# A gated linear attention and token/channel mixer kernel: some transposes moved from TensorE to transposing DMAs, with a new order of the program

## The chip, the cores and the metric

The kernel runs on one core of a Trainium2 chip. The metric is the device time of one execution in microseconds (us): lower is better, and the median of several executions is compared. A profile is one execution of the same program recorded by the hardware profiler.

The engines named below: TensorE (PE; its weight loads are listed as PEld) does matmuls and transposes, VectorE (DVE), ScalarE (ACT) and GpSimd (POOL) do elementwise work, SyncE (SP) issues DMAs. TensorE writes into eight PSUM banks only; VectorE and ScalarE take results out of them (an "eviction").

## What is computed

Four batches, 8 heads, 768 tokens, head size 48. First a recurrence with decay for each head, then an MLP mixer over tokens and over channels (d_tok 256, d_ch 1536, width 8 x 48 = 384):

```python
for t in range(S):
    state = alpha[:, :, t, :, None] * state + einsum('bhd,bhe->bhde', k[:, :, t], v[:, :, t])
    y[:, :, t] = einsum('bhd,bhde->bhe', q[:, :, t], state)
x = y.transpose(0, 2, 1, 3).reshape(B, S, H * D)
h = maximum(x.transpose(0, 2, 1) @ w_tok1, 0) @ w_tok2
u = x + h.transpose(0, 2, 1)
out = u + maximum(u @ w_ch1, 0) @ w_ch2
```

Inputs and output are float32; matmul operands in the kernel are bfloat16.

## The kernel before

The recurrence is done in chunks of 128 tokens, six to a batch, numbered 0 to 23 over the four batches (batch 2 has chunks 12 to 17). For a chunk done alone (`natural_chunk`; batch 0 and the first four chunks of batch 1 go in pairs, `paired_chunks`) the steps are:

- four loads on SP's queue: alpha, k, q, v of the chunk, 192 KB each (`natural_loads`, line 203);
- ScalarE: la = ln(alpha) (line 241); TensorE: cum, its running sum over the tokens, with four columns of totals (lines 345 and 348); ScalarE: ek = exp(-cum) and eq = exp(cum) (lines 254 and 256);
- POOL: the decayed keys pkk = k x ek and queries pkq = q x eq, and v cast to bfloat16 (lines 273 and 280);
- `s_transpose` (line 290): 16 TensorE transposes of 64x64 blocks (`row_tiles`, line 287) put pkk and pkq, transposed, into two PSUM banks, and two evictions (line 295) bring them to the tile tkq, [128, 2, 4, 128];
- gt: the products of keys and queries (line 362), masked on VectorE into gm (line 302); state (line 383) and its decay and sum (st, ss, lines 312 to 319); y = gm x v and the part from the state before (lines 395 and 331), evicted to x (line 326).

With a batch's six x tiles the mixer runs: tok1 (two groups of six matmuls, line 574) and relu to ht; tok2 (line 623) for each chunk, added to x on VectorE, which makes u (line 629). Then u is transposed in two halves of three chunks: 18 TensorE transposes a half (step `utp`, `row_tiles` again), and two evictions a half (line 641) into ut, [128, 3, 768]. (Batch 0 makes u's transpose directly by matmuls, `mixed`.) The channel mixer `channel` then does ch1 (24 groups of three matmuls that read ut, line 663; each evicted with relu to rt, lines 561 and 563) and ch2 (groups of four, line 687), adds u on VectorE (line 700) and stores 192 KB per chunk from SP's queue (line 703).

Every step is put into a list with `g.add` and is numbered by its place in it. The order in which the steps are issued is written out in the string `ORDER`: the step's number, after a point the PSUM banks that it uses, and a letter where the engine is chosen (A for ScalarE, D for VectorE, P for POOL). `f` and a digit is a filling matmul on zeros (line 762), which keeps TensorE busy where it would have nothing to do. A loop at the end emits the steps in this order; each engine runs its own in that order, and semaphores between the engines are added by the framework. All DMAs of the program take eight completion counters in turn, in the order of the string, so a DMA's issue also waits until the DMA eight places before it has landed. The costs given to `g.add` (such as `{"PE": 0.25}`) are a planner's and do nothing in the program.

So TensorE mixes the channel matmuls of one batch with the chunks of the next: while batch 2's chunks run, batch 1's ch1 and ch2 stand between their steps.

Of the kernel before, what the change touches and what calls it, by code (L numbers as in the profile page):

```python
# [16 lines left out]
N_BANKS = 8  # L17
FETCH, BLOCK, AHEAD, ARRIVES = 193, 256, 449, (4.5, 30.0, 3.0)

# [4 lines left out]
0 1 f0 2 f0 f0 f0 f0 f0 3 f0 f0 f0 f0 f0 4 28 f0 29 f0 f0 30.0 5 31.1 32 f2 f2 38 6 f2 35 f2 33 f2 f2 f2 39 f2 36 f2  # L24
40 f2 43.2 41 7 47.3 66 f4 34 f4 65 48 44 50A 49D f4 68.4 8 45A 67.5 46D 75 f6 51.67 69 77 54.10 76 53 f3 9 f3 70 f3
55 f3 72 f3 f3 f3 73 f3 f3 f3 78 f3 105 84.3 80.2 52 104 81 10 85 56 83A f7 106.7 42P 37A 86D 107.1 87A f4 11 82D
57.46 108 71 88.03 114 59 111 58.25 109 12 90 115 61 63 60A 116 f4 62 119.4 64A f3 89 91.32 14 f6 93 120 f6 f6 122A f6
112 f6 f6 121A f6 117 123.6 f5 92 79A 74P f5 16 124 f5 110 f5 125A 126D 94.50 18 96 113A 118P 127.24 97 130.13 20
95.76 129 13A 100 24 128 98 102 133.5 99A 101 142.4 131 166.2 135 15A 141.7 143 132 144 146 169.0 145 136 17A 134.13
259 103D 137 139 19P 147 138A 163.5 140D 148 f6 150 152 149 151 162A 172.6 178.1 161D 175.3 f4 f4 164 170 21A 22D 23P  # L30
167 260 165D 179 171A 176 168D 180A 173 177D 189.4 261 174A 181.7 190D 187.5 26A 27P 182D 191.0 262 188D 25A 197.2
192D 185.1 198D 153 217.3 186A 213.6 263 218D 221.4 264 214D 155 207.7 222D 265.5 208D 215.0 300 267 227.2 268 216D
270 266.1 228D 201.3 273 271 205.6 274 202D 203.4 206A 301 272 211.7 204A 275 193.5 154A 212D 195.0 302 194D 276 183.2
196D 209.1 184D 277 278.36 303 279 210A 269 223.4 156P 280D 281A 292.75 224A 157 282 283 294 225.0 284A 285D 199.2 304
296 219.1 159 305 200D 286.47 226A 297 289.36 220A 287 307.5 343 306.2 291 315 234.0 314 288 317 308 290 229.1 309 316
293.46 344 310 239.5 313 295A 158D 345 311 298 249.7 299A 346 312 160A 250 366 318 230 333.23 367 347 319.46 320 335
251 322A 368 321D 336 240 252A 369 235 339 348.2 340 253 231 349 354 350 236 232D 352 370 241 237D 233 351 323 353 324
242A 371.7 238 325D 326A 361.3 243 244.2 372 362 486 373 375 327.10 487 330.56 328 355.43 245 376 356A 488 331 357A
246 329 374 489 377 378.71 332 247A 358.45 254.3 379A 508 360 380A 359 255 490 381.02 334.67 248 382 337 364.5 383
338A 363 256 509 365A 510 341 384.1 257A 342D 491.4 497 385A 511 492 388.0 493 495 258 386.2 389D 512 496 531 532  # L40
504.6 513.5 387A 494 498.37 505 514 394.1 533 500A 499D 390.4 517 395 515 392.0 396.2 391 400.6 518 393 398.3 534
501.71 397 516 402.54 519 399 520.02 404A 554 403D 526.3 521A 401 412.5 522A 555 502 448.4 535 527 405.60 449A 556
523.27 503 528 536.3 407A 436.4 524 406A 557 506.1 537 525 428.0 538 438.2 577 540 507D 437A 529.6 413D 429A 444.7 578
439A 539 530D 542 446.3 558 445D 541 549.1 408.4 447A 550 410.5 409D 551 579 559.0 411A 442.2 561 440.6 580 443D 560
564 424.7 441A 454.3 600 425A 563 422.1 581 455D 420.4 601 423A 562 582.5 565 421A 543.02 602 584 566.67 544D 572.3
545A 416.1 567D 585 603 568A 573 434.4 587 583 430.0 435D 417A 720 546.62 574 431A 569.37 548 432.5 721 588 604 426.1
547 586 433A 450.4 722 571 427A 552.0 451A 570 605.2 723 553A 418.6 606 575.5 419D 607 452.7 609 576A 414.1 453A 461.4
742 610 415A 724 466.3 743 611 589.06 608 612.25 591A 590D 744 595.7 476.1 614D 613A 596 481.0 745 597 615.65 592.27
765 617 482 731 593 766 462 746 594 477 767 616 598.5 478 768 599A 618.2 479 456.7 788 619A 753 457 620.6 769 480
622.5 621A 789 458 623A 790 467 459 776 791 628.1 632.2 629 626.6 460 624.5 633 630.7 627 634.1 792 811 468 631 812  # L50
625 471.2 635 813 472 469 636.67 470 639.51 638A 637D 473 640D 799 641A 814 483 474 834 463 484 725.3 475 464 747.6
726 770.7 666.5 727 729 465 749 793.1 667D 678.2 748 485 771 728 648.0 730 679D 794 646.4 649D 795 664.3 815 751 835
647D 656.5 772 836 665D 816.6 752 657A 760.2 670.1 837 817 738.0 818 750 658.4 671D 774 838 732.73 739 659A 754.56
734D 839.1 773 733A 775 761 783.0 755A 684.4 756D 841 644.3 762 685D 840 668.7 645D 797 676.2 784 669A 682.5 677A 785
777.64 683A 757.13 778D 735.07 779A 796 662.2 798 759 652.5 737 663A 822 654.6 653A 736 820 800.43 655A 780.27 758
740.5 802A 819 806.0 781 843 686.6 741A 763.1 782 687A 829.3 842 688.2 764A 807 844 786.5 801D 689A 650.7 808 787D
803.61 651A 846.04 821 804 672.2 847A 805 674.5 848A 845 680.7 830 673A 849.60 675A 831 823.14 681A 851 809.3 824A
660.2 825D 810A 850 642.5 661A 710.7 643A 711 852.0 690.1 853A 700.4 826.36 691 828 705.2 827 706 707 832.5 708 701
833A 709 702 854.0 703 704 856.6 855A 692 857A 695.3 693 860.2 694 868.5 861 858.4 696 869 859 862.0 864.6 863 697 865
866.1 698 715.2 867 699 716 873.54 870.06 874A 875D 717 872D 882.3 871D 712 718 883A 719 884.1 713 904.4 885A 714  # L60
896.5 905A 914.6 897A 886.0 915A 902.2 887A 878.3 903A 916.7 879A 910.1 917A 912.4 911A 920.5 913A 890.6 921A 918.0
891A 880.2 919A 892.3 881A 898.7 893A 894.1 899A 876.4 895A 888.5 877A 944.6 889A 922.0 929.2 923A 900.3 908.7 901D
906.1 909A 930 907A 939.4 945 946 934.5 947 935 948 936 931 937 924.0 938 932 925 933 926 940 927 941 928 949.3 942
950 943 951 954.7 955 952 956 953 957 958
# [12 lines left out]
class Graph:  # L77
# [5 lines left out]
    def add(self, name, costs, emit, reads=(), writes=(), prio=0, dma=None, new=(), tail=0.0, rows=False, loose=False, n=0):  # L83
        self.ops.append(Op(costs, emit, new))
        return self.ops[-1]
# [6 lines left out]
def kernel(  # L92
# [96 lines left out]
    for t in la_t + pkq_t + pkk_t:  # L189
# [615 lines left out]
```

## Time and profile before

| | us |
|---|---|
| median of 3 runs (lowest, highest) | 174.58 (173.62, 174.63) |
| the profiled execution's own time | 174.98 |
| its span, first to last instruction | 173.2 |
| TensorE transposes of pkk, pkq and x in `row_tiles` (line 287), instructions | 112 + 112 + 108 |
| evictions of them: tkq on ScalarE / VectorE | 18 x 0.594 / 10 x 0.418 |
| evictions of them: ut on ScalarE / VectorE | 6 x 0.642 / 6 x 0.450 |
| POOL: pkk, pkq, each | 1.000, 1.029 |
| input load of a chunk, issue to landing, medians | 4.2 to 4.6 |

Lengths of matmuls in the group rows overlap (a 384-column matmul is listed with 326 ns, but the next starts 163 ns later); the pieces of the chain of work do not overlap, and prices of matmuls are best read there. In the slices, each digit is a tenth of the slice's 4.33 us. In the waits, the engine and line before the arrow waited for those behind it. "To landing" is from a DMA's issue to the arrival of its completion.

### The profile page before, as it was taken

The numbers are of one execution on the slowest core, as the hardware profiler recorded it, in microseconds if no ns is written. First come the engines' busy times: TensorE is split into PE (matmuls) and PEld (weight loads), VectorE is DVE, ScalarE is ACT, GpSimd is POOL, SyncE is SP. The second block draws the span as 40 slices with busy tenths as digits, with TensorE's granted clock in tenths as the row PEclk, the third lists the DMA queues.
The fourth block names the chain that finished last, engine by engine and source line by source line (L and its number), as shares of the span: only waits on it lengthen the run. The fifth ranks groups of instructions, "written<-read, shape, count | busy, mean of one in ns | idle before, by whom it ended". The sixth has DMA issues, their size and how long they took to land.

```text
span 173.2 us, 5139 instructions
## 1 busy us (share of the span) xinstructions
PE 166.3 (96%) x2095; PEld 106.1 (61%) x2095; DVE 98.8 (57%) x207; ACT 101.5 (59%) x213; POOL 70.7 (41%) x112
## 2 busy tenths in 40 slices
PE   7989799999999999899999999999999999999993
PEld 3667477555665666566566666666766666656662
DVE  3259786976843585697482718687972257101141
ACT  2577664757845767498896331688891212895000
POOL 7432511419494944928766111499950000000000
PEclk9999999999999999999999999999999999999999
DMA  5999999999999999989898999987000121200133
GB/s 139 261 262 265 251 338 406 285 262 315 244 312 169 204 250 186 237 159 200 162 193 141 206 165 218 229 228 132 0 4 0 45 95 45 91 4 0 44 119 109
DMA packets 86150, 30.20 MB, mean 174 GB/s; under 512 B 79600, under 2 KB 85104, under 8 KB 86128
## 3 DMA queue, kind: packets, MB, share of 16 engines
q1 hardware_dynamic: 86128, 29.89, 74.6%
q8 instruction: 16, 0.26, 0.7%
q14 instruction: 6, 0.05, 0.1%
HBM read 25.17 MB, written 4.72 MB: 172 GB/s over the span
## 4 chain that ended last, share of the span: by engine, by line
PE 69%; DMA 13%; issue 4%; SPq 4%; ACT 4%; POOL 3%; DVE 1%; ACTq 0%; POOLq 0%; DVEq 0%
PE bank L687 24%; PE bank L663 20%; DMA ina<-in_alpha_dram 9%; DMA rt_late<-in_moe_w_ch_dram 4%; SPq L203 4%; PE bank L762 3%; PE bank L287 2%; PE bank L623 2%; PE bank L574 2%; PE bank L362 2%; PE bank L493 2%; PE bank L331 1%; ACT la L241 1%; PE bank L395 1%; PE bank L554 1%
## 5 line engine op out<-in xcount | busy, mean ns | idle before, releaser
L663 PE MATMUL bank<-ut,wc 128*128 128x384 bf16 x288 | 51.8, 326 | 0.0
L663 PEld LDWEIGHTS <-wc 128*128 128x128 bf16 x288 | 26.4, 98 | 16.2 <-ACT wc L728 0.2
L273 POOL TENSOR_TENSOR pkk<-ink,ek 128x384 bf16<-128x384 f32 x24 | 23.9, 1000 | 15.6 <-ACT ek L254 13.2
L687 PE MATMUL bank<-wc,rt 128*128 128x384 bf16 x144 | 26.9, 326 | 0.2 <-ACT wc L734 0.2
L687 PE MATMUL bank<-wc,rt_late 128*128 128x384 bf16 (+2 forms) x156 | 25.2, 314 | 0.0
L561 ACT ACTIVATE rt_late<-bank 128x384 bf16<-128x384 f32 x40 | 19.2, 496 | 4.0 <-PE bank L663 4.0
L302 DVE TENSOR_TENSOR gm<-bank,u 128x512 bf16<-128x512 f32 x28 | 17.7, 682 | 5.8 <-PE bank L362 5.4
L241 ACT ACTIVATE la<-ina 128x384 bf16<-128x384 f32 x24 | 12.1, 526 | 14.1 <-DMA ina<-in_alpha_dram 14.0
L700 DVE TENSOR_TENSOR o<-bank,x 128x384 f32<-128x384 f32 (+2 forms) x19 | 10.2, 535 | 17.7 <-PE bank L687 17.4
L687 PEld LDWEIGHTS <-rt_late 128*128 128x128 bf16 x156 | 14.5, 98 | 8.3
L273 POOL TENSOR_TENSOR pkq<-inq,eq 128x384 bf16<-128x384 f32 x18 | 18.5, 1029 | 1.2 <-ACT eq L256 1.2
L687 PEld LDWEIGHTS <-rt 128*128 128x128 bf16 x144 | 13.2, 98 | 8.2 <-issue 0.4
L280 POOL CAST vb<-inv 128x384 bf16<-128x384 f32 x21 | 10.6, 506 | 17.7 <-DMA inv<-in_v_dram 13.0
L563 DVE TENSOR_SCALAR rt<-bank 128x384 bf16<-128x384 f32 x25 | 13.0, 556 | 4.2 <-PE bank L663 4.1
L762 PE MATMUL bank<-zeros 128*128 128x384 bf16 x57 | 13.9, 371 | 1.2 <-DVE la L190 1.2
L315 POOL TENSOR_TENSOR ss<-st,al 128x384 bf16<-128x384 f32 x12 | 10.0, 831 | 12.4 <-DVE st L312 7.3
L254 ACT ACTIVATE ek<-bank 128x384 f32<-128x384 f32 x24 | 11.3, 502 | 5.3 <-PE bank L348 3.0
L326 ACT CAST x<-bank 128x384 bf16<-128x384 f32 x18 | 8.5, 486 | 9.6 <-PE bank L331 8.5
L302 DVE TENSOR_TENSOR gm<-bank,pmask 128x512 bf16<-128x512 f32 x20 | 12.8, 684 | 2.0 <-PE bank L493 1.9
L561 ACT ACTIVATE rt<-bank 128x384 bf16<-128x384 f32 x23 | 10.9, 493 | 1.9 <-PE bank L663 1.7
L563 DVE TENSOR_SCALAR rt_late<-bank 128x384 bf16<-128x384 f32 x8 | 4.4, 553 | 13.1 <-PE bank L663 12.2
L295 ACT COPY tkq<-bank 128x512 bf16<-128x512 bf16 x18 | 9.9, 594 | 1.9 <-PE bank L287 1.8
(119 smaller groups left out, 238.3 us busy)
## 6 DMA issues: line engine op xcount, KB each, us to landing
out_dram<-o SPq DMA_DIRECT2D x23, 192.0 KB, 2.5
ina<-in_alpha_dram SPq DMA_DIRECT2D x14, 192.0 KB, 4.2
ink<-in_k_dram SPq DMA_DIRECT2D x14, 192.0 KB, 4.5
inq<-in_q_dram SPq DMA_DIRECT2D x14, 192.0 KB, 4.6
inv<-in_v_dram SPq DMA_DIRECT2D x14, 192.0 KB, 4.5
rt_late<-in_moe_w_ch_dram SPq DMA_DIRECT2D x2, 1152.0 KB, 10.9
rt_late<-in_moe_w_ch_dram SPq DMA_DIRECT2D x4, 576.0 KB, 6.8
ina<-in_alpha_dram SPq DMA_DIRECT2D x5, 384.0 KB, 6.3
```

The lines of the kernel that those rows point to most:

```text
L241: g.add("la", {"ACT": 0.43}, lambda e: act.activation(la[:, :, 0:D], t, AF.Ln), key, [u["la"][1]], pr + 5)
L254: g.add("ek", {"ACT": 0.38}, lambda e: act.activation(ek, banks[bank.place][:, 0:HD], AF.Exp, scale=-1.0), [bank], [kek], pr + 4)
L273: lambda e, dst=dst, src=src, ex=ex: {"POOL": gps, "DVE": dve}[e].tensor_tensor(dst[:, :, 0:D], src, ex().rearrange("p (h d) -> p h d", h= ...
L280: lambda e: evict[e](vb, src), ksrc, [u["vb"][1]], pr + 4)
L302: g.add("gm", {"DVE": 0.60}, lambda e: dve.tensor_tensor(gm, banks[bank.place].rearrange("p (j t) -> p j t", j=4), wide(mask, [[0, 4], lis ...
L315: g.add("ss", {"POOL": 0.79}, lambda e: gps.tensor_tensor(ss, st.rearrange("p (h d) -> p h d", h=H), wide(al, [[1, 8], [0, D]]), ALU.mult) ...
L561: act.activation(dst, src, AF.Relu)
L563: dve.tensor_scalar_max(dst, src, 0.0)
L663: pe.matmul(banks[bank.place][:, 0:HD], lhsT=wc1[wp][:, kc, off : off + 128], rhs=ut_t[b % 2][:, kc, cs], start=(kc == 0), stop=(kc == NM ...
L687: pe.matmul(banks[bank.place][:, 0 : hi - lo], lhsT=rt_t[(b * NDC + mc) % NRT][:, i * 128 : i * 128 + 128], rhs=wc2[:, mc, lo:hi], start=( ...
L700: g.add("o", {"DVE": 0.09 + 0.38 * width}, lambda e, i=i, bank=bank, o=o, lo=lo, hi=hi: dve.tensor_tensor(o[:, lo:hi], banks[bank.place][: ...
L762: pe.matmul(banks[place][:, 0:HD], lhsT=zeros[:, 0:128], rhs=zeros, start=True, stop=True, skip_group_check=True)
```

## The change

Two sets of steps are replaced by DMAs that transpose on the way from SBUF to SBUF, issued by ScalarE (`nc.scalar.dma_start_transpose`):

- `TRD`, chunks 12 to 17: in `s_transpose`, the 16 transposes and two evictions of a chunk become two DMAs, pkk and pkq into their halves of tkq (128 x 512 bfloat16, 128 KB each). 12 DMAs.
- `UTD`, batches 2 and 3: in `separate`, the 18 transposes and two evictions of a half of u become one DMA (128 x 1152 bfloat16, 288 KB). Four DMAs.

For this the x tiles of three chunks become one tile (`x_all`), and ut is laid out as [128, 6 chunks, 3, 128] instead of [128, 3, 768], so that ch1 reads three blocks of 128 columns. `natural_chunk` is split into `natural_front` (loads to products), the transpose and the rest, and `natural_run` puts them into the list in another sequence; the options `FUSE` and `TOT` are off.

`ORDER` is searched anew, so every engine's sequence differs, from the first chunks on: the string has 1006 items where it had 1016, and 61 filling matmuls where it had 57. Between the engines, evictions move: of the relu evictions of ch1, ScalarE has 64 (63 before) and VectorE 32 (33), but differently spread over the batches; x is evicted 14 times on ScalarE (18) and 10 on VectorE (6); three casts of the first weights go from ScalarE to POOL and one from POOL to VectorE, and two casts of the channel weights from ScalarE and one from POOL to VectorE. In the stretch where batch 2's chunks run, batch 1's ch2 comes earlier: it is issued before batch 2's tok1, and the first ch1 of batch 2 follows soon after tok2 of batch 2, behind three tile transposes, two states, three gt and a cum of batch 3's chunks. Before, 24 matmuls of ch2 stood between that tok2 and the end of u's transposes.

```diff
+UTD, TRD, TOT = (2,3), (12,13,14,15,16,17), False
...
-    x_t = many("x", NX, [128, HD])
+    x_all = many("x", 4, [128, 3, HD])
+    x_t = [x_all[n // 3][:, n % 3, :] for n in range(NX)]
...
-    ut_t = many("ut", 2, [128, NM, S])
+    ut_t = many("ut", 2, [128, NCH, NM, C])
...
+    def s_transpose(n, dst, key, prio):
+        u, tb = units[n], [Bank(), Bank()]
+        if n in TRD:
+            for i, w in enumerate("kq"):
+                src, ksrc = u["p" + w]
+                g.add("trd", {"ACT": 1.2}, lambda e, i=i, src=src: nc.scalar.dma_start_transpose(
+                    dst[:, i], src.rearrange("p h d -> p (h d)")), [ksrc], [(*key, i)], prio, late=2.0)
+            return
+        g.add("tr", {"PE": 0.25}, lambda e: row_tiles(tb, sources(n)), [u["pk"][1], u["pq"][1]], tb, prio, new=tb, rows=True)
+        s_transposed(n, tb, dst, key, prio)
...
+            if b in UTD:
+                x = x_all[(n0 + mine[0]) % NX // 3]
+                g.add("utd", {"ACT": 1.3}, lambda e, x=x, cs=cs: nc.scalar.dma_start_transpose(
+                    ut[:, cs].rearrange("p i j t -> p (i j) t"), x.rearrange("p i d -> p (i d)")), ku,
+                    [("ut", b % 2, j, part, h) for j in range(NM) for h in range(2)], 1000 * b + 170, late=3.0)
+                continue
...
-                              rhs=ut_t[b % 2][:, kc, cs], start=(kc == 0), stop=(kc == NM - 1),
+                              rhs=ut_t[b % 2][:, ti, kc, :], start=(kc == 0), stop=(kc == NM - 1),
```

More of the change, by code (lines that the diff above doesn't have):

```diff
@@ L81, in __init__, with add @@
         self.ops = []
-    def add(self, name, costs, emit, reads=(), writes=(), prio=0, dma=None, new=(), tail=0.0, rows=False, loose=False, n=0):
+    def add(self, name, costs, emit, reads=(), writes=(), prio=0, dma=None, new=(), tail=0.0, rows=False, loose=False, n=0, late=0.0):
         self.ops.append(Op(costs, emit, new))
@@ L287, in row_tiles, with sources, s_transposed @@
                 pe.transpose(banks[place[h].place].bitcast(BF16)[:, 64 * i : 64 * i + 64], src[rows], id128[rows, rows])
-    def s_transpose(n, dst, key, prio):
-        u, tb = units[n], [Bank(), Bank()]
-        srcs = [u["p" + w][0][:, 2 * j : 2 * j + 2, :] for w in "kq" for j in range(4)]
-        g.add("tr", {"PE": 0.25}, lambda e: row_tiles(tb, srcs), [u["pk"][1], u["pq"][1]], tb, prio, new=tb, rows=True)
+    def sources(n):
+        return [units[n]["p" + w][0][:, 2 * j : 2 * j + 2, :] for w in "kq" for j in range(4)]
+    def s_transposed(n, tb, dst, key, prio):
         for h in range(2):
@@ L355, in natural_chunk @@
         ktkq = [("tkq", i, h) for h in range(2)]
-        s_transpose(n, tkq, ("tkq", i), pr + 2)
         gb = [Bank(), Bank()]
+        tb = [Bank(), Bank()] if then else []
         def gt(e):
+            if then:
+                row_tiles(tb, sources(then))
             for j in range(4):
@@ L365, in gt @@
                               skip_group_check=True)
-        g.add("gt", {"PE": 0.235}, gt, ktkq, gb, pr + 1, new=gb, rows=True)
+        more = [units[then]["p" + w][1] for w in "kq"] if then else []
+        g.add("gt", {"PE": 0.47 if then else 0.235}, gt, ktkq + more, gb + tb, pr + 1, new=gb + tb, rows=True, n=24 if then else 8)
+        if then:
+            s_transposed(then, tb, tkq_t[then % NG], ("tkq", then % NG), pr + 1)
         for par in range(2):
@@ L602, in xt, with uT @@
                                   rhs=id128, start=(at == 0), stop=False, skip_group_check=True)
[L604 removed]
+                def uT(e, bank=bank, js=js, ts=ts):
                     for m in range(NDT):
[L606 removed]
+                        pe.matmul(banks[bank.place][:, 0:HD], lhsT=ht_t[b % 2 * NDT + m][:, js], rhs=wt2[:, m, ts],
                                   start=False, stop=(m == NDT - 1), skip_group_check=True)
@@ L612, in mixed @@
                 g.add("ut", ACT_OR_DVE, lambda e, j=j, bank=bank, cs=cs: evict[e](
-                    ut[:, j, cs], banks[bank.place][:, 0:HD]), [bank],
+                    ut[:, cs, j, :], banks[bank.place][:, 0:HD].rearrange("p (i t) -> p i t", t=C)), [bank],
                     [("ut", b % 2, j, part, h) for h in range(2)], 1000 * b + 170)
```

132 lines of the change are left out of this document (77 added, 55 removed).

## Prediction

> **What bounds the kernel now.** I read the page first (busy times, then the 40 slices), then TensorE's waits, then the chain of work in order of time, then the windows and the landing times of the stretch that changes.
>
> ```profile
> PE 166.3 (96%) x2095; PEld 106.1 (61%) x2095; DVE 98.8 (57%) x207; ACT 101.5 (59%) x213; POOL 70.7 (41%) x112
> PE   7989799999999999899999999999999999999993
> ACT  2577664757845767498896331688891212895000
> DMA  5999999999999999989898999987000121200133
> ```
>
> TensorE is busy 96% of the span and, but for the first slices, in every one of them: it is the bound, so TensorE work taken out comes off the end unless a wait takes its place. The DMA engines are full until about slice 27 (117 us); they are what can make such a wait. ScalarE is idle 41% on average, but slices 14 to 22, where batch 2 runs, show 7 to 9.
>
> ```profile
> PE bank L762 <- DVE la L190: 1.2, 1, 1.2
> PE bank L444 <- POOL pkk L273: 0.9, 1, 0.9
> PE bank L383 <- POOL pkk L273: 0.4, 1, 0.4
> PE bank L345 <- ACT la L241: 0.4, 1, 0.4
> ```
>
> All that TensorE waited for something by name comes to 3 us: there is little idle time to win back, and much that a late transfer could add.
>
> **Terms on TensorE.** The edit takes out 168 transposes of 64x64: 16 for each of six chunks of batch 2 (keys and queries), 18 for each half of u in batches 2 and 3. The chain gives groups of them:
>
> ```profile
> 84.81 0.57 PE bank L287 x32
> 107.62 0.63 PE bank L287 x36
> 144.94 0.63 PE bank L287 x36
> 20.30 0.97 PE bank L762 x6
> ```
>
> Two chunks take 0.57, so six take 1.71; u takes 0.63 a batch, 1.26 for two: 2.97 us gone. The new order has 61 filling matmuls for 57; at 0.97/6 = 0.16 each, the four cost 0.65 us where TensorE does not wait anyway, nothing where it does. I take 0.65. Twenty evictions of transposes leave ScalarE and VectorE too; neither sets the end, so I count them only in the queues below. The new layout of u makes ch1 read three blocks of 128 columns where it read 384 in a row. The first two of these rows are the nearest, the others (state, two gt, the within part of y) serve below:
>
> ```profile
> 110.30 0.16 PE bank L345
> 117.09 2.44 PE bank L663 x15
> 116.90 0.19 PE bank L383 x4
> 87.12 0.55 PE bank L362 x16
> 89.24 0.20 PE bank L395 x8
> ```
>
> L345 reads eight blocks of 48 in 0.16 us, L663 reads a straight 384 in 2.44/15 = 0.16: nothing (a 1% loss in 288 would be 0.5). Three casts of the first weights go from ScalarE to POOL:
>
> ```profile
> L734 ACT CAST wt<-ina x1: 833/833/833, 24.4 to 24.4; 128x768 bf16<-128x768 f32 x1
> L734 POOL CAST wt<-inv x1: 829/829/829, 27.5 to 27.5; 128x768 bf16<-128x768 f32 x1
> ```
>
> The same 0.83 us on either engine: nothing, or 0.8 if one were late for its first matmul.
>
> **Terms of the new DMAs.** No row shows a transposing DMA. Issue and landing are bounded by the plain DMAs; the last row is of 100 to 120 us, the other landings of the whole run.
>
> ```profile
> L203 SPq DMA_DIRECT2D ina<-in_alpha_dram x19: 368/702/2070, 0.8 to 111.3; - x19
> L203 SPq DMA_DIRECT2D ink<-in_k_dram x19: 384/906/3451, 1.3 to 115.4; - x19
> L203 SPq DMA_DIRECT2D inq<-in_q_dram x19: 646/1167/4218, 1.9 to 115.8; - x19
> L203 SPq DMA_DIRECT2D inv<-in_v_dram x19: 425/1278/2651, 8.8 to 116.6; - x19
> 90.42 2.45 SPq L203 DMA_DIRECT2D inv<-in_v_dram  x1
> out_dram<-o SPq DMA_DIRECT2D x23, 192.0 KB, 2.5
> ina<-in_alpha_dram SPq DMA_DIRECT2D x14, 192.0 KB, 4.2
> ina<-in_alpha_dram SPq DMA_DIRECT2D x5, 384.0 KB, 6.3
> out_dram<-o SPq DMA_DIRECT2D x6, 192.0 KB, 3.5
> ```
>
> Issue: 0.37 to 2.45 us (the longest of the single-chunk loads from 87 us on); I take 1.0, the mean of the four medians. Landing: 3.5 for a key or query tile (128 KB), 4.2 for half of u (288 KB), ends 2.5 and 6.3.
>
> *First chunk.* Behind the first cum of batch 2 ScalarE has ek, eq, la, then ht (which needs both tok1 groups, 12 matmuls, 2.0 us), and only then the keys' transpose: issue at 2.4, ek of the next chunk, queries' issue at 3.8, landed at 7.3. TensorE has 33 matmuls of 0.163 (tok1, tok2, ch1), two halves of batch 1's u (0.315 each), two states (0.19) and a cum (0.16, and 0.11 for its four columns) before gt, 6.7 us: it waits 0.6. The five later chunks have 3.5 to 6.7 us of TensorE work between issue and gt: covered, each at a cost of what its landing exceeds that.
>
> *ScalarE's queue.* From the first cum of batch 2 to gt of its fourth chunk the new order gives ScalarE 6 ek, 6 eq, 6 la, 8 rt, 1 ht, 1 o, 1 x, 1 ut and 11 issues.
>
> ```profile
> 67.55 0.50 ACT L254 ACTIVATE ek<-bank 128x384 f32<-128x384 f32 x1
> 67.94 0.50 ACT L256 ACTIVATE eq<-bank 128x388 f32<-128x388 f32 x1
> 77.91 1.30 ACT L561 ACTIVATE rt_late<-bank 128x384 bf16<-128x384 f32 x3
> L241 ACT ACTIVATE la<-ina 128x384 bf16<-128x384 f32 x24 | 12.1, 526 | 14.1 <-DMA ina<-in_alpha_dram 14.0
> 66.98:87.05 20.07, 18.95 (x259) 11.87 (x256) 13.59 (x28) 15.60 (x36) 13.44 (x21) 1.00 1.02 194
> 25.00:30.00 5.00, 5.00 (x86) 3.62 (x82) 3.83 (x8) 3.10 (x6) 0.83 (x1) 1.00 1.03 395
> 115.00:120.00 5.00, 4.93 (x93) 3.26 (x92) 3.78 (x9) 4.63 (x12) 5.00 (x9) 1.00 0.96 227
> ```
>
> ek starts 0.39 before eq, so 0.39 each; rt 0.43; la 0.53: 4.7 + 3.4 + 3.2 + 1.3 + 0.6 = 13.2 us, and 11 issues of t. TensorE has 116 matmuls of 0.163 in it, two halves of u, six cums, five states, three gt (0.28) and three y (0.37), 24.0, and 1.1 idle as now (20.07 less 18.95, the same stretch in the windows, whose columns are length, busy time of TensorE, its weight loads, VectorE, ScalarE and POOL, clock, DMA share and GB/s): 25.1. At t = 1.0 ScalarE has 24.2: nothing, but the cover is gone at t = 1.08, and each further 0.1 us costs 1.1. Behind a blocked issue stand la, ek, eq and rt; POOL's products and TensorE's free banks wait for those.
>
> *SP's loads.* Eight completion counters are shared in turn, so an issue also waits for the DMA eight back, and SP's loads now wait for transposes; 3.5 to 6.8 us of TensorE work lie between, about the landing: nothing. But eleven tiles of 128 KB (1.44 MB) share the engines: 3.7 us at 395 GB/s, 6.4 at 227, the ends that the windows show. The stretch has room for 20.07 x (1 - 194/227) = 2.9 us of it, so batch 3's loads run 0.8 to 3.5 us late. The new order asks for chunk 21's decay 6.2 us of work after its load's place; landing 4.2 and la 0.5 leave 1.5. Wait: 0 to 2.0, I take 0.7. The Trainium skill (DMA: Bandwidth & Descriptors, Issuing engines are not separate DMA queues) says that DMAs of all queues run on the same 16 engines and interleave: by it this term holds whichever queue issues, and if ScalarE's queue were apart it would be nothing.
>
> *Hand-over of batch 2.*
>
> ```profile
> 103.72 1.95 PE bank L623 x12
> 105.67 1.95 PE bank L687 x12
> 104.08 2.88 DVE L629 TENSOR_TENSOR x<-bank,x 128x384 bf16<-128x384 f32 x6 [0.42 <-PE bank L623]
> L295 DVE COPY tkq<-bank x10: 410/415/425, 71.4 to 128.5; 128x512 bf16<-128x512 bf16 x10
> L312 DVE TENSOR_TENSOR st<-bank,ss 128x384 f32<-128x384 f32 x12 | 6.6, 550 | 2.8 <-PE bank L514 1.9 <-POOL ss L315 0.7
> ```
>
> Now 24 matmuls of ch2 stand between tok2 and the end of u; in the new order batch 1's ch2 is spent before tok1, and between tok2 (1.95) and the first ch1 stand three tile transposes, two states, three gt and a cum: 4.3 us in all. VectorE adds u in 2.88/6 = 0.48 each, so the third chunk is ready 0.53 + 1.44 = 1.97 after tok2's start, and half of u lands at 1.97 + 4.2 = 6.2. TensorE waits 1.9. An early landing hardly helps, for VectorE is as late: its adds end at 3.41, four copies (0.42) and a state add (0.55) at 5.64, and a gt and a cum follow, 6.2. Low end 1.6 (landing 2.5, those five overlapping by 0.07 each as the adds do, 0.548 long and 0.48 apart); high end 4.0 (landing 6.3). Batch 3's halves have 4.6 and 5.0 us of ch2 and ch1 after their issue, with the queues quiet: nothing, or 1.7 at 6.3.
>
> **Sum.** -2.97 + 0.65 + 0.6 + 0.7 + 1.9 = +0.9 us on the profiled execution's 174.98: 175.9. That execution lies 0.4 above the median of the runs, 174.58, so I say 175.5 for the median. Its own range is 173.8 (fills and loads free, gap 1.6) to 176.8 (loads 2.0).
>
> **Rivals.**
> *The waits are hidden (faster).* Fills stand where TensorE waits (-0.65), the first gt finds its tile (-0.6), loads keep up (-0.7), the gap is 1.6 (-0.3) and today's 1.1 of idle goes: 175.5 - 3.4 = 172.1. For it: the few waits of now; against: the gap is VectorE's, whatever the DMA does.
> *ScalarE becomes the bound (slower).* Place: batch 2's stretch; it decides above t = 1.08. At t = 1.5: 13.2 + 16.5 - 25.1 = 4.6, of which 0.6 is counted: 179.5. For it: v's median of 1.28 and the full engines; against: 128 KB is less than 192.
> *The transposes land late (slower).* With the 6.3 of a 384 KB load: the first gt waits 3.4 (+2.8), the gap is 4.0 (+2.1): 180.4. The Trainium skill (VectorE: DVE Perf Modes, The three transpose paths) gives 1309 ns for 128x128 by the crossbar, 390 by TensorE; taken four times for a tile and nine for half of u, an estimate from that page, landings would be 5.2 and 11.8 and the sum near 192. No row here shows it.
> That the change does not do what it says can be excluded: the built program has the 16 transposing DMAs on ScalarE and 168 transposes fewer.
>
> **Chances.** My sum 0.48, hidden 0.25, ScalarE 0.17, late 0.10. About 1% (1.7 us) is what a measurement of this kernel tells from no change: faster below 172.8, slower above 176.3. Of hidden 0.22 is faster, 0.03 within; of my sum 0.36 within, 0.12 slower (what it leaves out above its range's end); the two slow ones lie above. So 0.22, 0.39, 0.39. The range for 8 in 10 reaches to the hidden case and to ScalarE's: 171.8 to 179.6.
>
> **What would show it.** Right: the group of 64x64 transposes of u down to 36 and of pkk to 64; TensorE idle some 2 us before the first ch1 of batch 2, released by the transposing DMA or by gt's copies; la of chunks 20 to 22 waiting for its input. Wrong: issues well over 1.1 us on ScalarE with rt and ek late behind them; a wait of ch1 in batch 3; or TensorE without a gap, when the time falls under 173.

## The result, and the profile after

The changed kernel is slower: 185.27 us in the median of four runs, where the kernel before had 174.61 on the same chip, a ratio of 1.049 (95% interval 1.043 to 1.055); in a second measurement 185.75 against 174.99, a ratio of 1.058 (1.047 to 1.068). The forecast was 175.5, with a range up to 179.6. Single executions stray upwards (the first profiled one of the changed kernel took 415.54 us, with every matmul about twice its usual time), so the ratios leave them out, the medians do not, and the profile after is that of the second measurement. Its own time is 185.87 us, its span 184.2.

From the page of the changed kernel: the busy times, TensorE's and ScalarE's slices, the granted clock, the DMA engines, and the two large queues (q10 holds the transposes).

```profile
PE 168.3 (91%) x1931; PEld 105.9 (57%) x1931; DVE 99.9 (54%) x207; ACT 90.2 (49%) x192; POOL 71.1 (39%) x113
...
PE   7979899999999998699896996879999999999993
...
ACT  3578424799647463362531123636976110688000
...
PEclk9999999999999999789999999686999999999999
DMA  6999999999999999999999999999500018310132
...
q1 hardware_dynamic: 86128, 29.89, 76.7%
q10 hardware_dynamic: 11264, 2.75, 11.7%
```

TensorE stands idle for 184.2 - 168.3 = 15.9 us, where it was 173.2 - 166.3 = 6.9. Its busy time has grown by 2.0 us although 168 transposes are gone: where it waits, the clock behind the wait falls. ScalarE, a rival's bound, is emptier in the stretch than before (issues of DMAs are not counted as busy), and the DMA engines are full one slice longer. Three windows of 20 us show where the time went: first the kernel before, then the changed one (columns as in the prediction: length, busy time of TensorE, its weight loads, VectorE, ScalarE, POOL, clock, DMA column, GB/s).

```profile
65.00:85.00 20.00, 18.88 (x288) 12.32 (x282) 13.31 (x26) 14.97 (x34) 12.80 (x19) 1.00 1.00 187
85.00:105.00 20.00, 20.00 (x248) 12.86 (x240) 10.56 (x20) 11.46 (x26) 8.18 (x13) 1.00 1.09 185
105.00:125.00 20.00, 19.93 (x292) 13.09 (x289) 16.12 (x34) 14.81 (x33) 14.39 (x23) 1.00 0.74 160
```

```profile
65.00:85.00 20.00, 17.56 (x181) 10.82 (x179) 12.05 (x25) 9.05 (x20) 8.66 (x14) 0.91 1.31 194
85.00:105.00 20.00, 17.30 (x182) 10.72 (x181) 12.64 (x24) 5.87 (x15) 10.59 (x16) 1.00 1.41 176
105.00:125.00 20.00, 15.95 (x186) 9.62 (x183) 11.57 (x23) 8.96 (x21) 10.76 (x17) 0.88 1.23 219
```

Of the 9.0 us more of idle time, 58.81 - 50.81 = 8.0 lie in these 60 us. The waits of the changed kernel say for what:

```profile
POOL vb L283 <- DMA inv<-in_v_dram: 20.1, 9, 6.2
ACT la L244 <- DMA ina<-in_alpha_dram: 19.2, 10, 3.6
ACT la L244 <- DMA tkq<-pkk: 6.0, 1, 6.0
PE bank L359 <- ACT la L244: 3.2, 2, 2.5
PE bank L402 <- DMA tkq<-pkq: 1.8, 1, 1.8
PE bank L712 <- ACT ut L690: 1.7, 1, 1.7
```

la waited 14.0 us for decay before, 19.2 now. The 6.0 us put down to a transposing DMA belong to this too: la reads no transposed tile, and its own load, issued at 98.54 us, takes 6.4 us to land, which is when la starts, at 105.03. TensorE's own waits are for la (cum, L359), once for a transposed tile (gt, L402) and once for a copy that stood behind an issue of 2.88 us in ScalarE's queue (ch1, L712). The last load, of v of chunk 23, is issued at 126.9 us, where the prediction's row has 116.6. In both kernels SP's queue has few gaps there: added up, the issues of the 44 loads of chunks 13 to 23 hold its queue for 41.9 us before and 52.4 now, 10.5 more, about as much as the last load is late. The issues and landings of the new DMAs, and the loads they run beside (first the queue rows: shortest, median and longest issue in ns; then the medians from issue to landing, in us):

```profile
L308 ACTq DMA_TRANSPOSE tkq<-pkk x6: 1204/1208/1443, 70.0 to 98.6; - x6
L308 ACTq DMA_TRANSPOSE tkq<-pkq x6: 1204/1261/2876, 71.7 to 99.8; - x6
L682 ACTq DMA_TRANSPOSE ut<-x x4: 1258/1578/2012, 118.4 to 153.7; - x4
```

```profile
ina<-in_alpha_dram SPq DMA_DIRECT2D x14, 192.0 KB, 5.7
...
tkq<-pkk ACTq DMA_TRANSPOSE x6, 5.8
tkq<-pkq ACTq DMA_TRANSPOSE x6, 5.7
ut<-x ACTq DMA_TRANSPOSE x4, 5.0
```

### The profile page after: what moved, and what is told of

Same layout as the page of the kernel before. It is cut to its first block, busy times and chain, and to the rows that moved or that the text cites. A ratio compares the mean times of both kernels' runs of the same rounds, so it can differ in the third digit from the quotient of the medians.

```text
span 413.8 us, 4807 instructions
## 1 busy us (share of the span) xinstructions
PE 409.5 (99%) x1931; PEld 190.6 (46%) x1931; DVE 103.8 (25%) x207; ACT 93.1 (22%) x192; POOL 70.2 (17%) x113
## 3 DMA queue, kind: packets, MB, share of 16 engines
q10 hardware_dynamic: 11264, 2.75, 4.3%
## 4 chain that ended last, share of the span: by engine, by line
PE 99%; ACT 0%; DVE 0%; issue 0%; DVEq 0%
PE bank L736 31%; PE bank L712 31%; PE bank L813 7%; PE bank L666 4%; PE bank L617 4%; PE bank L345 2%; PE bank L402 2%; PE bank L487 2%; PE bank L359 2%; PE bank L290 2%; PE bank L438 1%; PE bank L536 1%; PE bank L649 1%; PE bank L597 1%; PE bank L557 1%; PE bank L569 1%
## 5 line engine op out<-in xcount | busy, mean ns | idle before, releaser
L712 PE MATMUL bank<-ut,wc 128*128 128x384 bf16 x288 | 132.7, 683 | 0.3 <-ACT ut L690 0.3
L712 PEld LDWEIGHTS <-wc 128*128 128x128 bf16 x288 | 48.9, 174 | 67.5 <-issue 66.3
L736 PE MATMUL bank<-wc,rt 128*128 128x384 bf16 x144 | 69.2, 681 | 0.0
L736 PE MATMUL bank<-wc,rt_late 128*128 128x384 bf16 (+2 forms) x156 | 65.8, 653 | 0.0
L736 PEld LDWEIGHTS <-rt_late 128*128 128x128 bf16 x156 | 26.8, 176 | 35.1 <-issue 33.2
L749 DVE TENSOR_TENSOR o<-bank,x 128x384 f32<-128x384 f32 (+2 forms) x19 | 10.2, 537 | 102.9 <-PE bank L736 102.9
L813 PE MATMUL bank<-zeros 128*128 128x384 bf16 x61 | 30.9, 691 | 1.2 <-DVE la L193 1.2
L257 ACT ACTIVATE ek<-bank 128x384 f32<-128x384 f32 x24 | 11.8, 493 | 35.3 <-PE bank L362 17.7
L617 PE MATMUL bank<-x,wt 128*128 128x384 bf16 x36 | 16.8, 684 | 0.0
L666 PE MATMUL bank<-ht,wt 128*128 128x384 bf16 x36 | 16.5, 673 | 0.0
L813 PEld LDWEIGHTS <-zeros 128*128 128x128 bf16 x61 | 10.6, 180 | 11.9 <-issue 10.2
L606 DVE TENSOR_SCALAR rt<-bank 128x384 bf16<-128x384 f32 x15 | 8.4, 558 | 29.8 <-PE bank L712 29.8
L672 DVE TENSOR_TENSOR x<-bank,x 128x384 bf16<-128x384 f32 x18 | 9.9, 557 | 19.3 <-PE bank L666 19.3
```

The source lines that it names most:

```text
L257: g.add("ek", {"ACT": 0.38}, lambda e: act.activation(ek, banks[bank.place][:, 0:HD], AF.Exp, scale=-1.0), [bank], [kek], pr + 4)
L617: pe.matmul(banks[bank.place][:, 0:HD], lhsT=wt1[:, kc, m * 128 : m * 128 + 128], rhs=x_t[(n0 + kc) % NX], start=(kc == 0), stop=(kc == NC ...
L666: pe.matmul(banks[bank.place][:, 0:HD], lhsT=wt2[:, m, i * 128 : i * 128 + 128], rhs=ht_t[b % 2 * NDT + m], start=(m == 0), stop=(m == NDT ...
L672: g.add("u", {"DVE": 0.47}, lambda e, i=i, bank=bank: dve.tensor_tensor(x_t[(n0 + i) % NX], banks[bank.place][:, 0:HD], x_t[(n0 + i) % NX] ...
L712: pe.matmul(banks[bank.place][:, 0:HD], lhsT=wc1[wp][:, kc, off : off + 128], rhs=ut_t[b % 2][:, ti, kc, :], start=(kc == 0), stop=(kc == ...
L736: pe.matmul(banks[bank.place][:, 0 : hi - lo], lhsT=rt_t[(b * NDC + mc) % NRT][:, i * 128 : i * 128 + 128], rhs=wc2[:, mc, lo:hi], start=( ...
```

## The experiments

Three causes were held against each other: the traffic of the transposes delays the loads; their issues hold ScalarE's queue; the new order is slow by itself. A fourth, the lower clock, came from the profile. Each ratio below is to the kernel before, run on the same chip.

| kernel | median us | ratio (95% interval) |
|---|---|---|
| changed | 185.75 | 1.058 (1.047 to 1.068) |
| new order, all transposes on TensorE | 181.78 | 1.045 (1.037 to 1.053) |
| new order, u by DMA | 182.71 | 1.048 (1.043 to 1.054) |
| new order, keys and queries by DMA | 187.37 | 1.077 (1.069 to 1.084) |
| new order, TensorE, DMAs beside | 189.57 | 1.082 (1.075 to 1.089) |
| new order, TensorE, ScalarE copies instead | 182.93 | 1.043 (1.037 to 1.049) |
| new order, TensorE, plain DMAs beside | 186.94 | 1.065 (1.056 to 1.073) |
| changed, half of batch 3's loads | 178.51 | 1.017 (1.010 to 1.023) |
| new order, TensorE, half of batch 3's loads | 183.08 | 1.048 (1.042 to 1.054) |
| changed, 46 more fills | 186.07 | 1.069 (1.062 to 1.076) |
| new order, TensorE, hand-over covered | 182.60 | 1.039 (1.033 to 1.046) |
| old order, batch 3's u by DMA | 174.00 | 0.998 (0.995 to 1.002) |
| old order, DMAs beside | 184.42 | 1.060 (1.052 to 1.067) |
| old order, ScalarE copies instead | 187.36 | 1.075 (1.067 to 1.083) |
| old order, DMAs beside, half of batch 3's loads | 185.95 | 1.066 (1.059 to 1.073) |

**The changed kernel again**, unedited:

> The changed kernel itself, once more, for a profile that can be laid beside the one before: its first profile shows every matmul of TensorE about twice as long as in the kernel before, from the first to the last, which no other execution of it shows in its time. Expected: 182 to 186 us, as in its other executions. If ScalarE's queue is the bound (its issues over 1.1 us): issue rows of 1.5 us and more in batch 2's stretch, rt and ek late behind them, TensorE idle 5 us or more there. If the transposes land late: gt and ch1 of batch 2 and ch1 of batch 3 wait for the transposing DMAs, landings over 5 us. If the loads come late: la of batch 3's chunks waits for its input and cum for la, 3 us or more. If it is the new order by itself, waits of TensorE that name none of these three.

It gave the profile above. ScalarE's busy time and issue times (mostly 1.2 us) speak against the issues as the bound; late loads are what most of the waits name.

**The order and the two parts.** Transposes go back to TensorE, with one bank for each engine's eviction, put in where two banks are free ahead of the first user; the items of the DMAs are dropped from the string. For both, for the keys and queries only, and for u only:

```diff
-                g.add("trd", {"ACT": 1.2}, lambda e, i=i, src=src: nc.scalar.dma_start_transpose(...
+            def by_pe(e):
+                row_tiles(tb, sources(n))
+                for h, on in ((0, "ACT"), (1, "DVE")):
+                    evict[on](...)
+            extra.append((by_pe, tb))
```

> The changed kernel with all 16 transposing DMAs taken back: the 168 transposes are on TensorE again (in the new layout of u and in the new order, each group put in where its first user needs it), and ScalarE and VectorE evict them, one bank each. If the new order itself costs the time (the early ch2 of batch 1, the other spread of evictions), it stays near the changed kernel, 183 to 187 us. If the DMAs cost it, by their issues on ScalarE, by their landing or by what they take from the loads, it falls to 173 to 177 us, with la's waits for decay back near 14 us and TensorE idle about 7 us.

> The changed kernel with only the four DMAs of u (batches 2 and 3); the keys and queries of batch 2 are transposed on TensorE. If what costs is the load stream losing DMA time to transposes, this has two of fourteen in the full stretch, about 4.4 of 16 us of engine time: 176 to 178 us. If ScalarE's held queue costs, it has 4 of 16 issues: 176 to 178. If the wait for half of u at the hand-over of batch 2, with the clock lost after it, is the main cost, 179 to 181. If the order costs, 183 or more.

> The changed kernel with only the twelve DMAs of batch 2's decayed keys and queries; u is transposed on TensorE. If lost load traffic or ScalarE's held queue costs the time, it stays at 181 to 185 us, with la waiting for decay 17 us or more. If the hand-over's wait for half of u is the main cost, it falls to 177 to 180.

No single cause is enough, and none of these three kernels fell in a range expected of it. Without any DMA the new order is at 1.045, where the changed kernel was at 1.049 and 1.058: most of the loss is there already, and the intervals overlap, although the changed kernel has 3 us of TensorE work less. Keys and queries alone by DMA are clearly slower (1.077); u alone by DMA is not to be told from the order alone (1.048). Why keys and queries alone are slower than both parts together is open. What the order alone loses can be seen at the hand-over of batch 2, in the windows and TensorE's waits of the kernel with all transposes on TensorE:

```profile
110.00:115.00 5.00, 4.08 (x81) 2.75 (x79) 3.90 (x9) 3.13 (x8) 4.67 (x8) 1.00 1.12 221
115.00:120.00 5.00, 3.31 (x69) 2.17 (x69) 4.46 (x10) 2.47 (x6) 3.37 (x6) 0.81 1.01 182
```

```profile
PE bank L409 <- ACT tkq L298: 1.2, 1, 1.2
...
PE bank L433 <- ACT ut L694: 0.7, 1, 0.7
PE bank L409 <- ACT tkq L309: 0.7, 1, 0.7
PE bank L728 <- ACT tkq L309: 0.7, 1, 0.7
```

TensorE is idle 2.6 us there and has a mean clock of 0.81 in the second window. The first wait shown is there, for an ordinary eviction (L298), and so is the second, for one of u put in by hand (L694); the other two, for evictions by hand (L309), come before, at 84 and 75 us. Over the whole run this kernel has 3.8 us more of idle time than the kernel before and 2.8 us more of busy time. So its 7 us are the new order with transposes that its search did not place, not a pure price of the order.

**DMAs that nobody waits for.** All transposes on TensorE and the 16 DMAs as well, into scratch tiles; first with a slip (both halves of u into one tile, so that the second issue waited for the first landing), then without it:

```diff
-                    dst[:, i], src.rearrange("p h d -> p (h d)")), ...
+                    beside[n % 2][:, i], src.rearrange("p h d -> p (h d)")), ...
```

> All 168 transposes on TensorE as in the kernel of the order alone, and the 16 transposing DMAs issued as well, at their places on ScalarE's queue with the same sources, but into tiles that nothing reads. So the traffic, the issues and the completion counters are as in the changed kernel, and nobody waits for a landing except those that share a counter. If the landing of a tile that gt or ch1 needs is what costs, it is near the order alone, within 2 us. If issues on ScalarE or traffic taken from the loads cost, it is 6 us or more above the order alone: 180 to 188 us; then la's waits tell the two apart: by traffic the loads land late, by ScalarE's queue la starts late though its load has landed.

The kernel with the slip has 191.51 us, a ratio of 1.098 (1.090 to 1.106).

> The kernel with all transposes on TensorE and the 16 transposing DMAs beside them, mended: the two halves of u go to two scratch tiles. In the kernel before it both went to one, so that the second issue waited for the first landing and held ScalarE, and TensorE waited 4.8 us at 128 us for a copy behind it. Without that, 185 to 188 us if issues or traffic cost something by themselves; 181 to 183 if all of its extra time came from that mistake.

So the cost needs nobody who waits for a landing: DMAs that nothing reads cost 6.5 us over the order alone by the ratios (1.082 and 1.045); the median, 189.6, lies above the range expected. Then one of the two suspects at a time: ScalarE's time without traffic, and traffic without transposing.

```diff
-                g.add("trd", {"ACT": 1.2}, lambda e, ...: nc.scalar.dma_start_transpose(...
+                g.add("trd", {"ACT": 1.2}, lambda e, ...: [act.copy(beside[n % 2][:, :, i], ...) for _ in range(2)]
```

> All 168 transposes on TensorE, no transposing DMA; in the place of each DMA on ScalarE's queue stand copies that read the same source and take ScalarE about as long as an issue (two of 128x512 for a tile of keys or queries, one of 128x1152 for half of u), into scratch tiles. What is left of the kernel with the DMAs beside is ScalarE's time alone, without traffic and without completion counters. If ScalarE's held queue costs the time: within 1 us of the kernel with the DMAs beside, 185 to 188. If the traffic does: 181 to 183, like the order alone.

```diff
+                g.add("trd", {"ACT": 1.2}, lambda e, ...: nc.scalar.dma_start(beside[n % 2][:, :, i], ...
```

> All transposes on TensorE; in the place of each transposing DMA ScalarE issues a plain copy of the same source to a scratch tile, in rows of 256 bytes, so with the same bytes and about as many packets. If transposing itself makes the DMAs dear (slow packets that hold the loads), it falls to 181 to 183; if any DMA of this size at this place costs as much, it is within 1 us of the kernel with the transposing DMAs beside, 185 to 188.

Held for as long, without DMAs, ScalarE costs nothing that can be told from the order alone (1.043 and 1.045); plain DMAs cost about 3.5 us (1.065), and transposing ones about 3 more (1.082). The plain ones also take half the issue time (0.63 to 0.65 us against 1.2), so it is not sure that this difference comes from the transposing itself. When the last load of v is issued, and how long la waits for decay, go with the result; the rows of the order alone, of ScalarE's copies, and of the transposing DMAs beside:

```profile
L206 SPq DMA_DIRECT2D inv<-in_v_dram x19: 454/982/2662, 8.7 to 117.0; - x19
...
ACT la L244 <- DMA ina<-in_alpha_dram: 4.8, 5, 2.3
```

```profile
L207 SPq DMA_DIRECT2D inv<-in_v_dram x19: 457/882/2813, 8.8 to 119.7; - x19
...
ACT la L246 <- DMA ina<-in_alpha_dram: 4.9, 3, 2.5
```

```profile
L207 SPq DMA_DIRECT2D inv<-in_v_dram x19: 466/1147/2862, 8.7 to 126.7; - x19
...
ACT la L246 <- DMA ina<-in_alpha_dram: 11.2, 6, 5.4
```

SP's issues say the same: the 44 loads of chunks 13 to 23 hold its queue for 42.1 us in the order alone and 42.5 beside the copies, but 51.7 beside plain DMAs and 53.0 beside transposing ones.

**The loads taken away**, in the changed kernel, and as a control in the order alone:

```diff
-            got["op" + w] = load_input(t, src[b, :, ts : ts + C, :]...
+            hs = slice(0, 4 if b == 3 else 8)
+            got["op" + w] = load_input(t[:, hs], src[b, hs, ts : ts + C, :]...
```

> The changed kernel, with the loads of batch 3's chunks (18 to 23) cut to the first four of the eight heads; the other half of those tiles keeps what earlier chunks left there, so the output is not the reference's. That takes 2.36 MB away from the stretch in which the transposes move 2.1 MB, with the same number of DMAs, issues and counters. If the transposes cost by delaying the loads: la's waits for decay fall from 19 us to under 15, the 2.5 us wait of the cum at 116 us and the wait of the gt at 100 us go, and the time falls to 177 to 181. If ScalarE's held queue costs, it stays at 184 to 186.

> Control for the run with half the loads of batch 3: the kernel of the order alone, with the same half of the heads of chunks 18 to 23 not loaded (output not the reference's). If the loads bound only the kernels with DMAs, it stays at 180.5 to 182 us, and the 7 us that the changed kernel won by the cut are the transposes' doing. If the loads bind the order alone as well, it falls to 177 to 179 and the cut says little of the transposes.

The changed kernel wins 6 to 7 us (its ratio falls from 1.049 and 1.058 to 1.017), the control none (1.045 and 1.048). With the loads halved, the changed kernel is faster than the order alone, by about 3%: there the DMAs bring a gain over the same order with TensorE's transposes. Its windows show TensorE busier again and the DMA column down in the third:

```profile
85.00:105.00 20.00, 19.06 (x195) 11.93 (x193) 13.22 (x25) 8.40 (x19) 11.17 (x17) 1.00 1.37 182
105.00:125.00 20.00, 18.73 (x276) 12.39 (x275) 15.67 (x32) 12.55 (x29) 14.39 (x22) 1.00 0.66 144
```

Not all that was expected of this kernel came. TensorE's wait for la is gone, and la's waits for decay fall to 10.4 us, but gt still waits for transposed queries, 0.9 us at 98 us and 2.6 us for the first tile of batch 2:

```profile
PE bank L403 <- DMA tkq<-pkq: 3.5, 2, 2.6
```

And it is still 1.7%, about 3 us, above the kernel before: that part is not the loads of batch 3.

**The clock.** Fills in six waits of the changed kernel, for example 15 ahead of the cum at 116 us:

```diff
-... 764.4 770 759.5 748 783.0 ...
+... 764.4 770 759.5 748 f2 f2 f2 f2 f2 f2 f2 f2 f2 f2 f2 f2 f2 f2 f2 783.0 ...
```

> The changed kernel with 46 more filling matmuls (7.5 us of TensorE) put into six places where its TensorE waits: 10 ahead of the ch1 at 75.7 us (wait 1.7), 4 ahead of the cum at 88.0 (0.7), 11 ahead of the gt at 99.9 (1.8), 15 ahead of the cum at 116.0 (2.5), 3 and 3 ahead of two gt at 121.9 and 123.2 (0.5, 0.6). They compute nothing that is used. If the clock that is granted falls because TensorE stood idle, the rows at 0.66 to 0.84 go to 1.0 and up to 4.3 us come back: 181.5 to 183.5. If the low clock has another cause, or the fills push later work, 185 to 187.

```profile
PE 172.2 (94%) x1977; PEld 108.7 (59%) x1977; DVE 99.1 (54%) x207; ACT 90.5 (49%) x192; POOL 71.2 (39%) x113
...
PEclk9999999999999999999999999999999999999999
```

The clock is full in every slice, and without the 46 fills (46 x 0.163 = 7.5 us) TensorE is busy 164.7 us, 3.6 less than in the changed kernel. The time does not fall (1.069, against 1.049 and 1.058), and the loads come hardly earlier: the last one is issued at 126.1 us, 126.9 in the changed kernel. So winning the clock back gains nothing here; the lost clock was a companion of the waits, not what set the time.

**Cover at the hand-over**, in the order alone: 16 matmuls of ch2 moved behind tok2.

```diff
-... 628.3 742.20 ... 753.67 ... 796.1 ... 771.53 ...
+... 628.3 468 742.20 ... 753.67 456.5 ... 796.1 457 ... 771.43 458 ...
```

> The kernel of the order alone with four groups of ch2 of batch 1 (16 matmuls, 2.6 us) taken from ahead of batch 2's tok1 to between its tok2 and the gt of batch 3, as cover for the hand-over; the other groups move up into their places. If the bare hand-over is the order's cost, the idle time of 2.6 us at 113 to 118 us and the low clock behind it go: 177 to 179 us. If the order loses its time elsewhere, or the cover is only missed earlier, 181 to 183.

It is not faster in a measurable way (1.039 and 1.045, overlapping). That what is moved there is missing earlier is likely, but was not shown.

**The part with quiet queues**: the old order, only batch 3's u by DMA, with six ch2 groups of batch 2 gathered between tok2 and ch1.

```diff
-... 857A 695.3 693 860.2 694 868.5 861 858.4 696 869 859 ... 873.54 870.06 874A 875D 717 872D 882.3 ...
+... 857A 693 694 860.2 861 858.4 859 862.0 863 870 868.5 ... 867 873 695.3 696 697 698 715.2 716 ... 884.1 ...
```

> The kernel before with one part of the change: only the two halves of batch 3's u go by DMA, in the old order but for one place: tok2 of batch 3 in one run, then the six groups of batch 2's ch2 that are left, as cover, then ch1 of the half that lands first. No loads are left in the queues there. If the DMA is free where the queues are quiet and the cover is long enough, the 0.63 us of transposes come off: 173.8 to 174.3 where the kernel before has 174.6. If the landing or the layout costs, 174.6 or more.

The page's busy times, the group of ch1, the queue of the transposes (packets, MB, share of 16 engines) and the landing:

```profile
PE 165.7 (96%) x2059; PEld 105.7 (61%) x2059; DVE 98.6 (57%) x204; ACT 100.1 (58%) x212; POOL 70.7 (41%) x112
```

```profile
L674 PE MATMUL bank<-ut,wc 128*128 128x384 bf16 x288 | 51.8, 326 | 0.1
```

```profile
q10 hardware_dynamic: 2368, 0.59, 1.9%
...
ut<-x ACTq DMA_TRANSPOSE x2, 3.7
```

TensorE has 166.3 - 165.7 = 0.6 us less to do and waits for no transposed tile; ch1 takes 326 ns as before, so three blocks of 128 columns cost nothing. The time, 174.0 against 174.2, has an interval that holds 1, so that a version faster than both kernels is not shown.

**The old order.** Do the DMAs cost there too? 12 of them (keys and queries of batch 2) beside the TensorE transposes, each pair issued behind that chunk's evictions; then ScalarE copies in their place; then the DMAs with half the loads of batch 3.

```diff
+                extra.append(lambda e, i=i, src=u["p" + w][0]: nc.scalar.dma_start_transpose(
+                    beside[n % 2][:, i], src.rearrange("p h d -> p (h d)")))
```

> The kernel before, in its old order and with all transposes on TensorE, and beside them 12 transposing DMAs of batch 2's decayed keys and queries into scratch tiles that nothing reads; ScalarE issues each pair behind the evictions of that chunk's TensorE transposes, when the sources are long ready. If the traffic taken from the loads costs in any order, it is 178 to 181 us, with la's waits for decay above 14 us and loads that land later than 4.6 us. If the old order's deeper cover hides late loads and 14 us of issues, 174.5 to 176, and the new order has made the kernel sensitive to them.

> The old order with two ScalarE copies of 128x512 in the place of each of the 12 transposing DMAs (no traffic, no counter). If ScalarE's time alone made the 10 us of the kernel with the DMAs beside in the old order, it is 182 to 185 us; if the traffic and what the issues wait for made them, 174.5 to 178.

> The old order with the 12 transposing DMAs beside, and half of the heads of chunks 18 to 23 not loaded (output not the reference's). If the loads that the transposes delay made the 10 us, it falls from 184.4 to 175 to 179; if ScalarE's queue did, it stays above 182.

Here it is another cause. The DMAs cost more than either case expected (184.4), copies without traffic more still (187.4, also above what was expected; 1.075 against 1.060), and half the loads bring nothing (1.066). The 44 loads of chunks 13 to 23 hold SP's queue for 40.4 us beside these DMAs, no longer than before (41.9). The windows of the kernel with copies, and TensorE's longest wait:

```profile
65.00:85.00 20.00, 16.26 (x223) 10.55 (x218) 11.93 (x24) 16.08 (x33) 9.41 (x14) 0.91 1.11 192
85.00:105.00 20.00, 16.29 (x189) 10.09 (x187) 7.71 (x16) 16.85 (x36) 9.35 (x14) 0.83 1.00 160
...
PE bank L367 <- ACT tkq L300: 3.1, 2, 1.7
```

The old order gives ScalarE 14.97 + 11.46 = 26.4 us of work in these 40 us (the rows of before above); with 12 issues of 1.24 an estimate is 41.3, more than there is. In fact the stretch grows and ScalarE is not full in it (32.9 of 40 us with the copies); its results come late. TensorE waits by name for its evictions to tkq (3.1 us) and for its ek, la and eq (2.3, 1.7 and 1.0). In the changed kernel ScalarE has 9.05 + 5.87 = 14.9 there, and with the issues 29.8; in that order copies cost nothing. So the new order has room for the issues, and the DMAs cost through the loads; in the old order they cost through ScalarE's time.

## Why the prediction was wrong, step by step

| step | forecast us | what the runs showed |
|---|---|---|
| transposes off TensorE | -2.97 | right as far as tested: 0.6 of busy time for one batch's u, where 0.63 was said |
| first gt of batch 2 | +0.6 | its place moved: ch1 at 75.7 waits 1.7 for a copy behind an issue of 2.88; with half the loads the first gt itself waits 2.6 |
| SP's loads late, chunk 21's cum | 0.8 to 3.5 late, wait 0 to 2.0, taken 0.7 | last load 10.2 late, that cum waits 2.5; half the loads win 6 to 7 |
| hand-over of batch 2 | +1.9 | 1.5 for copies and u (see below; the 2.5 for la just ahead belongs to the loads) |
| ScalarE bound above t = 1.08 | 0 | t is 1.21 to 1.26, and still no bound: copies as long as the issues cost nothing that can be told |
| tail, batch 3's u | 0 | right, in the changed kernel and alone |
| new layout of ch1 | 0 | right: 326 ns, as before |

The step that failed is the one on SP's loads: taken at 0.7 us, it cost 6 to 7 by the half-load runs. The place was right: the cum that waits for la of chunk 21 is the longest wait that TensorE has (2.53 us), followed by the hand-over:

```profile
115.98 0.32 PE L359 MATMUL bank<-la,u 128*128 128x384 bf16 x1 [2.53 <-ACT la L244]
...
121.85 0.73 PE L402 MATMUL bank<-tkq 48*128 48x128 bf16 x16 [0.53 <-DVE tkq L298]
123.19 0.40 PE L402 MATMUL bank<-tkq 48*128 48x128 bf16 x8 [0.61 <-ACT tkq L298]
...
124.51 2.10 PE L712 MATMUL bank<-ut,wc 128*128 128x384 bf16 x6 [0.35 <-DMA ut<-x]
```

The size was wrong, and part of the reason can be named. First, the room: 2.9 us of it were read off GB/s (194 where 227 had been seen), but the same row has the DMA column at 1.02, so by busy time there was none. Second, the rate: the transposes were charged by bytes at 227 to 395 GB/s, what all DMAs together moved in other windows. By the time that their packets took they moved 2.75 MB in 11.7% of 184.2 us, 21.6 us of all 16 engines: 127 GB/s, where the loads and stores (q1 above) come to 211 by the same sum. At 127 the eleven tiles take 1.44 MB / 127 GB/s = 11.3 us, so the loads would come 8.4 us late with the room and 11.3 without; the trace has 10.2. This is an estimate, for packets share the engines (the DMA column goes up to 1.41), and 127 is no fixed rate: for u alone in quiet queues the sum gives 0.59 MB in 1.9% of 172.6 us, about 180 GB/s. A stream that is late by 8 to 11 us is no longer one wait at chunk 21; it can hold every step from 85 to 125 us that needs a load. That the cost goes through the loads, the half-load runs show. Whether it is time on the DMA engines or the shared counters was not separated. From 70 to 130 us SP's queue waited for DMAs by name for 1.0 us only, which speaks for the engines but does not settle it:

```profile
SPq L206 <- DMA inq<-in_q_dram: 0.8, 1, 0.8
...
SPq L206 <- DMA ink<-in_k_dram: 0.2, 1, 0.2
```

The Trainium skill (DMA: Bandwidth & Descriptors, Issuing engines are not separate DMA queues) was cited for DMAs of all queues running on the same engines; the trace agrees, with ScalarE's DMAs putting off SP's last load from 117.0 to 126.7 us.

A second omission: the order's own price was taken as four fills and one gap, +2.6 us; the order without DMAs lies 7 us above the kernel before, and the changed kernel with half the loads still 3 us above it. The 6 to 7 us of the loads and these 3 make up the slowdown of 4.9 to 5.8%. How much of the 7 belongs to the order and how much to transposes set in by hand stays open.

Two rows of before were misread, without weight in the sum: ScalarE's slices 14 to 22 show 3 to 9, not 7 to 9, and TensorE's waits by name add up to 3.5 us, not 3.

The rivals: that all is hidden was false wherever loads run, true in the tail. ScalarE as the bound was the right thought for the old order, where copies alone cost 12 us; in the new order the condition t > 1.08 was met and the price did not come: with its issues ScalarE has 29.8 of 40 us there. Late landing came true in size (5.7 to 5.8 for a tile, 5.0 for half of u, against 3.5 and 4.2), yet landings that no one waits for cost as much. Of the signs, the waits of la for its input were there; the wait of ch1 in batch 3 that would have spoken against the sum was not. The Trainium skill's page VectorE: DVE Perf Modes (The three transpose paths) gave an estimate of 5.2 for a tile, near the measured 5.8, and of 11.8 for half of u, which the measured 5.0 does not bear out.

## What to carry to other kernels

A DMA is hidden only if its engines have time to spare, and that is to be read from their busy share, not from the GB/s that other windows reached with other DMAs. When DMA engines are full, ask not who waits for the new transfer but which load comes later by it, and how many waits hang on that stream. And take away one resource at a time: the same DMAs cost through the loads in one order and through ScalarE in the other.

## What the runs showed of the hardware

- In the changed kernel ScalarE's queue is held 1.21 to 1.26 us (medians; longest 2.88) by the issue of a transposing DMA of 128x512 bfloat16, and in the kernel with plain DMAs 0.63 to 0.65 by one of the same bytes in its place.
- The landing of a transposing DMA did not grow with its size here: 5.7 to 5.8 us for 128 KB and 5.0 for 288 KB in the changed kernel's full queues, 3.7 for 288 KB in quiet ones (batch 3's u alone). That of the plain DMAs in their place did: 4.2 to 4.9 and 6.0.
- Behind waits of 1.7 and 2.5 us the granted clock fell to 0.66 and 0.68 in windows of 5 us of the changed kernel. These are means: from 76 to 79 and from 117 to 120 us it is 0.50, and so it is from 124 to 127, behind waits of 0.5 and 0.6. Filling matmuls in the waits kept it at 1.00, and the kernel gained nothing from it.

```profile
75.00:80.00 5.00, 4.35 (x42) 2.34 (x42) 2.31 (x6) 1.69 (x5) 1.99 (x3) 0.66 1.41 196
...
115.00:120.00 5.00, 4.02 (x32) 1.98 (x32) 2.89 (x6) 3.20 (x8) 3.22 (x5) 0.68 1.04 274
```
